# 64-row score matmuls of two experts side by side, three products of high and low parts, and eight buffers for turned probabilities

## The chip, the cores and the metric

The kernel runs on one core of one Trainium2 chip. The metric is device time in microseconds of one launch. TensorE (PE) multiplies, VectorE (DVE), ScalarE (ACT) and GpSimd (POOL) do the elementwise work, and SyncE (SP) issues the transfers.

## The reference, cut to what matters

Three stages follow each other on 2 batches of 768 tokens: a retention layer of 8 heads of 64, a channel MLP (512 to 2048 to 512), and a mixture of 4 attention experts of width 64. The change is in the last one:

```python
for e in range(E):                       # 4 experts, Hd = 64
    q = x @ wq[e]; k = x @ wk[e]; v = x @ wv[e]
    scores = scale * (q @ k.transpose(0, 2, 1))       # 768 x 768 for each batch
    scores = np.where(causal, -1000000000.0, scores)
    a = np.exp(scores - scores.max(-1, keepdims=True))
    a /= a.sum(-1, keepdims=True) + 1e-09
    ye = a @ v @ wo[e]
    # each token adds ye of its two best experts, weighted by the gate
```

## The kernel before

Matrix products keep more digits than one pass gives: an operand is split into a high part, rounded to the format that the program calls float32r, and the low part that is left, and products of parts are summed in PSUM.

In the attention stage `q_proj` (line 745) computes queries or keys of two experts (a pair p) for 384 tokens: 12 float32r matmuls of 128x384 in two groups of 6 (line 754). The 128 rows of the result are 64 of each expert. They leave by half-height instructions. For the queries ACT writes the high part into the expert's own 64 rows of a tile `QS` (line 764) and DVE the low part into the other 64 rows (line 766). For the keys ACT writes `KH` (771), DVE `KL` (773), and a DMA on SP copies each to the other 64 rows, so both halves hold the same.

`a_scores` (line 839) then makes the scores of one expert for 128 queries with matmuls over all 128 rows: `QS` against `KH` (line 861) and against `KL` (line 862), which sums all four products of parts. With nk = 128 to 768 keys there are 2 matmuls up to 512 keys, and 4 of half the width (320 or 384 columns) for 640 and 768. A score tile lies in one bank of PSUM (`ps1`) or two (`ps2`, three places). Behind it DVE masks the diagonal block (868) and finds the maximum (869), ACT takes the exponent with its sum (871), DVE inverts the sum (877, 878), and POOL scales by it and the gate (883). `a_turn` (889) transposes the 128x128 blocks on PE (903) and ACT or DVE copies them out (335) into `pt` or `ptn`. `a_value` multiplies by the values, two experts side by side in 64 columns each (922), and `a_out` applies the output weights (946). The value matmuls and transposes are plain float32, which the trace shows as two instructions for each value matmul and one for each transpose.

The retention stage has a similar form to the new one: at line 433 two heads are multiplied by 64-row float32 matmuls, one head in rows 0 to 63 and the other in rows 64 to 127.

The order on each engine isn't written out. `Plan.issue` lists the steps greedily: at each moment an engine that its own cost table calls free takes the waiting step of lowest priority number that has its inputs and whose buffers fit. So new costs and new buffer needs move the order of the whole attention stage.

Of the kernel before, what the change touches and what calls it, by code (L numbers as in the profile page):

```python
# [207 lines left out]
def region(base, size, n, space="S"):  # L208
    return [(space, base + i * size, size) for i in range(n)]
# [3 lines left out]
def retention_channel_mlp_mixture_attention(ctx: ExitStack, tc: tile.TileContext, a):  # L213
# [77 lines left out]
    x = o_h - 2 * (4 * KB + 16)  # L291
    PL["wv"] = PL["mraw"] = region(x, 4 * KB + 16, 2)
    PL["vraw"] = region(o_u, 4 * KB + 16, 1)
    PL["qk0"] = region(o_r, 3 * KB, 12)
    PL["vv0"] = region(o_r + 36 * KB, KB, 6)
    PL["ob"] = region(o_r + 42 * KB, 2 * KB, 2)
    PL["qk1"] = region(o_h, 3 * KB, 12)
    PL["vv1"] = region(o_h + 36 * KB, KB, 6)
    PL["pr"] = region(o_xt, 3 * KB, 8)
    PL["pt"] = region(o_x, 6 * KB, 3)  # L300
    PL["ptn"] = region(o_x, 7 * KB // 2, 5)
    PL["at"] = region(o_x + 18 * KB, 2 * KB, 3)
    PL["sm"] = region(o_sm, 16, 8)
    PL["mv"] = region(o_sm + 128, 16, 4)
# [10 lines left out]
    def new(n):  # L315
        return Buf(PL[n], n)
# [4 lines left out]
    def ACT(c, fn, r=(), w=()):  # L321
        P.add({"A": c}, lambda e: fn(), r, w)

    def DVE(c, fn, r=(), w=()):
        P.add({"V": c}, lambda e: fn(), r, w)
# [14 lines left out]
    def act_c(n):  # L340
        return 0.06 + n * 0.84e-3
# [391 lines left out]
        h, l, w = MW[n]  # L733
        return f32r(l if lo else h)[:, k * w + c0:k * w + c1]

    QS, KH, KL, VV, LG, GT = {}, {}, {}, {}, {}, {}
    xkeys = lambda t: [(t, "k", k) for k in range(NK)]

    def q_alloc(b):
        for e in range(E):  # L740
            QS[b, e], KH[b, e], KL[b, e] = (new(f"qk{b}") for _ in range(3))
        for t in range(NC):
            VV[b, t] = new(f"vv{b}")

    def q_proj(b, j, n, p):
        cs = slice(j * TB, (j + 1) * TB)
        pa = new("ps")
        xh, xl = XH[b][j], XL[b][j]
        for hf in range(2):
            def mm(hf=hf):  # L750
                i = 6 * hf
                for k in (2 * hf, 2 * hf + 1):
                    for lo, xt in ((0, xh), (0, xl), (1, xh)):
                        pe.matmul(f32(pa, TB), lhsT=mw(n, lo, k, p * 128, (p + 1) * 128), rhs=blk(f32r(xt))[:, k],  # L754
                                  start=(i == 0), stop=(i == 11))
                        i += 1
            PE(0.98, mm, r=list(MW[n][:2]) + xkeys(xh) + xkeys(xl) + ["seven"], w=[pa])
        for z in range(2):
            e = 2 * p + z
            own = slice(64 * z, 64 * z + 64)  # L760
            oth = slice(64 - 64 * z, 128 - 64 * z)
            if n == "wq":
                q = QS[b, e]
                ACT(0.39, lambda q=q, own=own: act.activation(f32r(q)[own, cs], f32(pa, TB)[own], AF.Copy, scale=0.125),
                    r=[pa], w=[(q, j, 0)])
                DVE(0.47, lambda q=q, own=own, oth=oth: dve.scalar_tensor_tensor(
                    f32r(q)[oth, cs], f32(pa, TB)[own], 0.125, f32(q)[own, cs], op0=OP.mult, op1=OP.subtract),
                    r=[pa, (q, j, 0)], w=[(q, j, 1)])
            else:
                kh, kl = KH[b, e], KL[b, e]  # L770
                ACT(0.39, lambda t=kh, own=own: act.activation(f32r(t)[own, cs], f32(pa, TB)[own], AF.Copy),
                    r=[pa], w=[(kh, j, 0)])
                DVE(0.47, lambda t=kl, h=kh, own=own: dve.tensor_tensor(f32r(t)[own, cs], f32(pa, TB)[own],
                                                                        f32(h)[own, cs], OP.subtract),
                    r=[pa, (kh, j, 0)], w=[(kl, j, 0)])
                for t in (kh, kl):
                    DMA(96e3, lambda t=t, own=own, oth=oth: sp.dma_start(f32(t)[oth, cs], f32(t)[own, cs]),
                        r=[(t, j, 0)], w=[(t, j, 1)])

    def q_val(b, t):  # L780
        j, cc = divmod(t, TPB)
# [57 lines left out]
    def a_scores(b, qt, p):  # L839
# [2 lines left out]
        sm = new("sm")  # L842
        PR = []
        P.bias -= (20, 40)[b]
        for z in range(2):
            e = 2 * p + z
            s, pr = new("ps2" if nk > 512 else "ps1"), new("pr")
            PR.append(pr)

            ways = 1 if nk <= 512 else 2  # L850
            wide = nk // ways

            def halves(ap, step):
                return ap[:, :ways * step].rearrange("p (a x) -> p a x", a=ways)[:, :, :wide]

            def mm(e=e, s=s):
                q = f32r(QS[b, e])[:, qt * C:(qt + 1) * C]
                for n in range(ways):
                    ks = slice(n * wide, (n + 1) * wide)
                    out = f32(s)[:, 512 * n:512 * n + wide]  # L860
                    pe.matmul(out, lhsT=q, rhs=f32r(KH[b, e])[:, ks], start=True, stop=False)  # L861
                    pe.matmul(out, lhsT=q, rhs=f32r(KL[b, e])[:, ks], start=False, stop=True)  # L862
            PE(2 * ways * max(0.107, wide * .4513e-3 + .015), mm, r=[(QS[b, e], j, 0), (QS[b, e], j, 1)] +
               [(t, jj, y) for t in (KH[b, e], KL[b, e]) for jj in range(j + 1) for y in range(2)], w=[s])

            def mx(s=s, z=z):
                end = 512 * (ways - 1) + wide
# [239 lines left out]
```

## Time and profile before

| | |
|---|---|
| three runs | 452.94, 453.08, 454.92 us, median 453.08 |
| profiled execution, its own time | 452.99 us |
| its span | 451.0 us |
| PE, PE's weight loads | 440.5 us, 416.2 us (98%, 92%) |
| DVE, ACT, POOL | 328.2, 223.3, 209.0 us (73%, 50%, 46%) |

The attention stage runs from 329.9 us to the end. A matmul's recorded duration includes the filling of a pipeline, so matmuls overlap in the records: what one costs PE is the distance from its start to the next one's start, called its step here. Start and duration of a row are its first two numbers.

### The profile page before, as it was taken

The page shows a single profiled execution, that of the slowest core. Times are in us where ns is not written, and L with a number is a line of the kernel's source. Part 1 is how long each engine was busy: PE and PEld are TensorE (multiplying, and loading weights), DVE is VectorE, ACT ScalarE, POOL GpSimd, SP SyncE. Part 2 cuts the span into 40 slices and gives each one's busy share as a digit, 9 for nine tenths or more (in the row PEclk, how much of TensorE's full clock was granted, in tenths as well). Part 3 has the DMA queues.
Part 4 walks back from the last instruction along what each step waited for, and adds up shares of the span by engine and source line. Part 5 has one row for each costly group of instructions (what it writes and reads, how often), then busy time and mean ns, then how long its engine had stood idle before and what let it go on. Part 6 is the DMA issues. An engine that isn't in the chain of part 4 may idle for free.

```text
span 451.0 us, 8469 instructions
## 1 busy us (share of the span) xinstructions
PE 440.5 (98%) x3200; PEld 416.2 (92%) x3200; DVE 328.2 (73%) x709; ACT 223.3 (50%) x467; POOL 209.0 (46%) x216
## 2 busy tenths in 40 slices
PE   8999999999999999999999999999999999999996
PEld 7778889999999999999999999999999987897885
DVE  2798786868659867876868665569657988878962
ACT  1477467164256336344354164244534756645852
POOL 1688768978989315326145064100401333224440
PEclk9999999999999999999999999999999999999999
DMA  7998923203104103114021002002230221101111
GB/s 267 331 366 322 322 69 124 94 8 133 47 1 140 48 1 120 68 48 139 2 89 53 1 1 93 2 0 95 70 72 18 66 67 39 49 1 47 49 49 47
DMA packets 14985, 40.11 MB, mean 89 GB/s; under 512 B 2272, under 2 KB 4960, under 8 KB 14944
## 3 DMA queue, kind: packets, MB, share of 16 engines
q1 hardware_dynamic: 14944, 39.57, 25.7%
q8 instruction: 25, 0.41, 0.4%
q14 instruction: 16, 0.13, 0.1%
HBM read 33.27 MB, written 3.15 MB: 81 GB/s over the span
## 4 chain that ended last, share of the span: by engine, by line
PE 86%; DVE 7%; POOL 2%; issue 1%; ACT 1%; DMA 1%; SPq 0%; DVEq 0%; ACTq 0%; POOLq 0%
PE ps L609 29%; PE ps L670 19%; PE ps L590 7%; PE ps L754 6%; PE ps L922 4%; PE ps L791 4%; PE ps L903 4%; PE ps L946 3%; PE ps L461 2%; PE ps L484 2%; PE ps L861 2%; PE ps L862 2%; PE ps L433 1%; DVE sm L869 1%; DMA vk<-in_vk_dram 1%
## 5 line engine op out<-in xcount | busy, mean ns | idle before, releaser
L609 PE MATMUL ps<-h,w 128*128 128x384 f32 x768 | 145.6, 335 | 0.7 <-DVE xT L613 0.4
L609 PEld LDWEIGHTS ps<-h,w 128*128 128x128 f32 x768 | 134.0, 188 | 1.4 <-DVE xT L613 0.7
L613 DVE TENSOR_TENSOR xT<-xT,ps 128x384 f32<-128x384 f32 x112 | 60.2, 550 | 36.9 <-PE ps L609 36.5
L883 POOL TENSOR_SCALAR pr<-pr,sm,gate 128x384 f32<-128x384 f32 (+5 forms) x48 | 34.7, 733 | 80.7 <-DVE ps L868 33.0
L546 POOL TENSOR_TENSOR w<-wy,w 128x512 fp32r<-128x512 f32 x26 | 33.6, 1297 | 44.3 <-PE ps L609 39.7
L670 PE MATMUL ps<-t,S 128*128 128x384 f32 x216 | 43.1, 334 | 0.0
L871 ACT ACTIVATE pr<-ps,sm 128x384 f32<-128x384 f32 (+5 forms) x48 | 30.4, 636 | 20.7 <-DVE sm L869 15.4
L677 ACT ACTIVATE u<-ps 128x384 f32<-128x384 f32 x36 | 17.6, 490 | 41.5 <-PE ps L670 35.8
L670 PEld LDWEIGHTS ps<-t,S 128*128 128x128 f32 x216 | 37.9, 188 | 0.1
L521 ACT ACTIVATE wx<-raw 128x512 f32<-128x512 f32 x32 | 21.5, 672 | 27.8 <-DVE ps L525 19.7
L590 PE MATMUL ps<-x,w 128*128 128x384 f32 x192 | 34.9, 336 | 0.4 <-ACT wx L521 0.4
L590 PEld LDWEIGHTS ps<-x,w 128*128 128x128 f32 x192 | 33.2, 188 | 0.8 <-ACT wx L521 0.6
L869 DVE TENSOR_REDUCE sm<-ps 128x1 f32<-128x384 f32 (+5 forms) x48 | 30.0, 625 | 2.9
L670 PE MATMUL ps<-x,w 128*128 128x384 f32 x144 | 28.8, 334 | 0.0
L685 ACT ACTIVATE h<-ps 128x384 fp32r<-128x384 f32 x36 | 17.6, 490 | 22.5 <-PE ps L609 14.4
L522 POOL TENSOR_SCALAR wx<-wx 128x512 f32<-128x512 f32 x32 | 20.1, 629 | 18.5 <-ACT wx L521 17.8
L670 PEld LDWEIGHTS ps<-x,w 128*128 128x128 f32 x144 | 25.3, 188 | 0.0
L545 ACT ACTIVATE w<-wy 128x512 fp32r<-128x512 f32 x26 | 16.3, 629 | 16.4 <-PE ps L609 16.1
L903 PE MATMUL ps<-ident,pr 128*128 128x128 f32 x168 | 22.4, 274 | 2.0 <-DVE at L933 1.1
L523 DVE TENSOR_SCALAR ps<-wx 128x512 uint32<-128x512 uint32 x32 | 22.0, 688 | 2.2 <-POOL wx L522 1.8
L527 DVE SCALAR_TENSOR_TENSOR wy<-raw,ps 128x512 uint32<-128x512 uint32 x32 | 21.8, 683 | 1.9 <-POOL w L546 1.3
L525 DVE SCALAR_TENSOR_TENSOR ps<-wx,ps 128x512 uint32<-128x512 uint32 x32 | 22.3, 695 | 1.1
(123 smaller groups left out, 878.4 us busy)
## 6 DMA issues: line engine op xcount, KB each, us to landing
raw<-in_w_dram SPq DMA_DIRECT2D x32, 512.0 KB, 3.4
vk<-in_vk_dram SPq DMA_DIRECT2D x12, 512.0 KB, 5.8
kq<-in_kq_dram SPq DMA_DIRECT2D x11, 512.0 KB, 5.7
qk<-qk SPq DMA_DIRECT2D x32, 96.0 KB, 2.1
out_dram<-ob SPq DMA_DIRECT2D x11, 256.0 KB, 2.0
tabY<-in_tabY_dram SPq DMA_DIRECT2D x6, 256.0 KB, 4.9
vraw<-in_wv_dram SPq DMA_DIRECT2D x1, 520.0 KB, 3.3
kq<-in_kq_dram SPq DMA_DIRECT2D x2, 256.0 KB, 3.0
```

What stands on the lines that cost most here:

```text
L523: DVE(0.62, lambda: dve.tensor_scalar(u32(z), u32(x), 4, 1, op0=OP.logical_shift_left, op1=OP.logical_shift_right), r=[x], w=[z])
L525: DVE(0.7, lambda: dve.scalar_tensor_tensor(u32(z), u32(x), 0x80000000, u32(z), op0=OP.bitwise_and, op1=OP.bitwise_or), r=[x, z], w=[z])
L546: POOL(1.34, lambda: pool.tensor_tensor(f32r(l), f32(y), f32(h), OP.subtract), r=[y, h], w=[l])
L590: pe.matmul(f32(pa, TB), lhsT=wt, rhs=blk(f32r(xt[b][j]))[:, k], start=(n == 0), stop=(n == 11))
L609: pe.matmul(f32(pa, TB), lhsT=wt, rhs=t, start=(n == 0), stop=(n == 5))
L613: DVE(0.55, lambda: dve.tensor_tensor(blk(f32(xt))[:, k], blk(f32(xt))[:, k], f32(pa, TB), OP.add), r=[pa] + [(xt, cc, w) for cc in range( ...
L670: pe.matmul(f32(pa, TB), lhsT=wt, rhs=t, start=(first and n == 0), stop=(n == 5), skip_group_check=True)
L754: pe.matmul(f32(pa, TB), lhsT=mw(n, lo, k, p * 128, (p + 1) * 128), rhs=blk(f32r(xt))[:, k], start=(i == 0), stop=(i == 11))
L869: dve.tensor_reduce(f32(sm)[:, z:z + 1], halves(f32(s), 512), axis=mybir.AxisListType.XY, op=OP.max, negate=True)
L871: ACT(act_c(nk) + .18, lambda s=s, pr=pr, z=z: act.activation(halves(f32(pr), wide), halves(f32(s), 512), AF.Exp, bias=f32(sm)[:, z:z + 1] ...
L883: POOL(0.28 + nk * 0.95e-3, lambda pr=pr, z=z, e=e: pool.tensor_scalar(f32(pr, nk), f32(pr, nk), f32(sm)[:, 6 + z:7 + z], GT[b, j][:, cc, ...
L903: pe.transpose(f32(pa)[:, i * C:(i + 1) * C], f32(PRS[z][x])[:, j * C:(j + 1) * C], ident)
```

## The change

`q_proj` leaves a pair by one full-height ACT instruction (high) and one full-height DVE instruction (low), for queries and keys alike; expert z stays in rows 64z to 64z+63. The copies by DMA are gone. `a_scores` computes both experts of a pair in one step of PE: for each of three products (high-high, low-high, high-low; low-low is dropped) one 64-row matmul for each expert, alternating, each into its own score tile. The step takes both score tiles at once, where before each expert took its own. Query and key tiles shrink from 12 to 8 places, and the places for `ptn` grow from 5 to 8 out of that.

```diff
--- before.py
+++ after.py
@@ -291,14 +291,14 @@
     x = o_h - 2 * (4 * KB + 16)
     PL["wv"] = PL["mraw"] = region(x, 4 * KB + 16, 2)
     PL["vraw"] = region(o_u, 4 * KB + 16, 1)
-    PL["qk0"] = region(o_r, 3 * KB, 12)
+    PL["qk0"] = region(o_r, 3 * KB, 8)
     PL["vv0"] = region(o_r + 36 * KB, KB, 6)
     PL["ob"] = region(o_r + 42 * KB, 2 * KB, 2)
-    PL["qk1"] = region(o_h, 3 * KB, 12)
+    PL["qk1"] = region(o_h, 3 * KB, 8)
     PL["vv1"] = region(o_h + 36 * KB, KB, 6)
     PL["pr"] = region(o_xt, 3 * KB, 8)
     PL["pt"] = region(o_x, 6 * KB, 3)
-    PL["ptn"] = region(o_x, 7 * KB // 2, 5)
+    PL["ptn"] = region(o_x, 7 * KB // 2, 5) + region(o_r + 24 * KB, 7 * KB // 2, 3)
     PL["at"] = region(o_x + 18 * KB, 2 * KB, 3)
     PL["sm"] = region(o_sm, 16, 8)
     PL["mv"] = region(o_sm + 128, 16, 4)
@@ -733,12 +733,13 @@
         h, l, w = MW[n]
         return f32r(l if lo else h)[:, k * w + c0:k * w + c1]
 
-    QS, KH, KL, VV, LG, GT = {}, {}, {}, {}, {}, {}
+    QK, VV, LG, GT = {}, {}, {}, {}
     xkeys = lambda t: [(t, "k", k) for k in range(NK)]
 
     def q_alloc(b):
-        for e in range(E):
-            QS[b, e], KH[b, e], KL[b, e] = (new(f"qk{b}") for _ in range(3))
+        for p in range(2):
+            for n in ("wk", "wq"):
+                QK[n, b, p] = new(f"qk{b}"), new(f"qk{b}")
         for t in range(NC):
             VV[b, t] = new(f"vv{b}")
 
@@ -755,27 +756,15 @@
                                   start=(i == 0), stop=(i == 11))
                         i += 1
             PE(0.98, mm, r=list(MW[n][:2]) + xkeys(xh) + xkeys(xl) + ["seven"], w=[pa])
-        for z in range(2):
-            e = 2 * p + z
-            own = slice(64 * z, 64 * z + 64)
-            oth = slice(64 - 64 * z, 128 - 64 * z)
-            if n == "wq":
-                q = QS[b, e]
-                ACT(0.39, lambda q=q, own=own: act.activation(f32r(q)[own, cs], f32(pa, TB)[own], AF.Copy, scale=0.125),
-                    r=[pa], w=[(q, j, 0)])
-                DVE(0.47, lambda q=q, own=own, oth=oth: dve.scalar_tensor_tensor(
-                    f32r(q)[oth, cs], f32(pa, TB)[own], 0.125, f32(q)[own, cs], op0=OP.mult, op1=OP.subtract),
-                    r=[pa, (q, j, 0)], w=[(q, j, 1)])
-            else:
-                kh, kl = KH[b, e], KL[b, e]
-                ACT(0.39, lambda t=kh, own=own: act.activation(f32r(t)[own, cs], f32(pa, TB)[own], AF.Copy),
-                    r=[pa], w=[(kh, j, 0)])
-                DVE(0.47, lambda t=kl, h=kh, own=own: dve.tensor_tensor(f32r(t)[own, cs], f32(pa, TB)[own],
-                                                                        f32(h)[own, cs], OP.subtract),
-                    r=[pa, (kh, j, 0)], w=[(kl, j, 0)])
-                for t in (kh, kl):
-                    DMA(96e3, lambda t=t, own=own, oth=oth: sp.dma_start(f32(t)[oth, cs], f32(t)[own, cs]),
-                        r=[(t, j, 0)], w=[(t, j, 1)])
+        hi, lo = QK[n, b, p]
+        c = 0.125 if n == "wq" else 1.0
+        ACT(act_c(TB), lambda: act.activation(f32r(hi)[:, cs], f32(pa, TB), AF.Copy, scale=c), r=[pa], w=[(hi, j)])
+        if n == "wq":
+            DVE(dve_c(TB), lambda: dve.scalar_tensor_tensor(f32r(lo)[:, cs], f32(pa, TB), c, f32(hi)[:, cs],
+                                                            op0=OP.mult, op1=OP.subtract), r=[pa, (hi, j)], w=[(lo, j)])
+        else:
+            DVE(dve_c(TB), lambda: dve.tensor_tensor(f32r(lo)[:, cs], f32(pa, TB), f32(hi)[:, cs], OP.subtract),
+                r=[pa, (hi, j)], w=[(lo, j)])
 
     def q_val(b, t):
         j, cc = divmod(t, TPB)
@@ -842,26 +831,26 @@
         sm = new("sm")
         PR = []
         P.bias -= (20, 40)[b]
+        ways = 1 if nk <= 512 else 2
+        wide = nk // ways
+        SS = [new("ps2" if nk > 512 else "ps1") for _ in range(2)]
+        (kh, kl), (qh, ql) = QK["wk", b, p], QK["wq", b, p]
+
+        def halves(ap, step):
+            return ap[:, :ways * step].rearrange("p (a x) -> p a x", a=ways)[:, :, :wide]
+
+        def mm():
+            for n in range(ways):
+                for i, (x, y) in enumerate(((qh, kh), (ql, kh), (qh, kl))):
+                    for z in range(2):
+                        zs = slice(64 * z, 64 * z + 64)
+                        pe.matmul(f32(SS[z])[:, 512 * n:512 * n + wide], lhsT=f32r(x)[zs, qt * C:(qt + 1) * C],
+                                  rhs=f32r(y)[zs, n * wide:(n + 1) * wide], start=(i == 0), stop=(i == 2))
+        PE(3 * ways * max(0.107, wide * .4513e-3 + .015) + 0.15, mm,
+           r=[(qh, j), (ql, j)] + [(t, jj) for t in (kh, kl) for jj in range(j + 1)], w=SS)
         for z in range(2):
-            e = 2 * p + z
-            s, pr = new("ps2" if nk > 512 else "ps1"), new("pr")
+            s, pr = SS[z], new("pr")
             PR.append(pr)
-
-            ways = 1 if nk <= 512 else 2
-            wide = nk // ways
-
-            def halves(ap, step):
-                return ap[:, :ways * step].rearrange("p (a x) -> p a x", a=ways)[:, :, :wide]
-
-            def mm(e=e, s=s):
-                q = f32r(QS[b, e])[:, qt * C:(qt + 1) * C]
-                for n in range(ways):
-                    ks = slice(n * wide, (n + 1) * wide)
-                    out = f32(s)[:, 512 * n:512 * n + wide]
-                    pe.matmul(out, lhsT=q, rhs=f32r(KH[b, e])[:, ks], start=True, stop=False)
-                    pe.matmul(out, lhsT=q, rhs=f32r(KL[b, e])[:, ks], start=False, stop=True)
-            PE(2 * ways * max(0.107, wide * .4513e-3 + .015), mm, r=[(QS[b, e], j, 0), (QS[b, e], j, 1)] +
-               [(t, jj, y) for t in (KH[b, e], KL[b, e]) for jj in range(j + 1) for y in range(2)], w=[s])
 
             def mx(s=s, z=z):
                 end = 512 * (ways - 1) + wide
```

What this does to the order on PE, first in batch 0 between the projections: `x` and `wk`, `wq` are inputs and weights of a projection, `qk0` are queries and keys of batch 0, `ps` is PSUM. Before:

```order
L754 MATMUL ps_71<-x_47_341,wk_470_3107 128x384
L754 MATMUL ps_71<-x_44_327,wk_472_3118 128x384
L861 MATMUL ps_71<-qk0_505_3477,qk0_513_3526 128x384
L862 MATMUL ps_71<-qk0_509_3494,qk0_513_3526 128x384
L754 MATMUL ps_71<-x_44_327,wk_470_3107 128x384
L754 MATMUL ps_71<-x_47_341,wk_470_3107 128x384
```

After, where "x2" is one 64-row matmul for each expert:

```order
L755 MATMUL ps_71<-x_47_341,wq_473_3126 128x384
L755 MATMUL ps_71<-x_44_327,wq_474_3135 128x384
L847 MATMUL ps_71<-qk0_504_3474,qk0_509_3508 128x384 x2
L847 MATMUL ps_71<-qk0_504_3474,qk0_510_3510 128x384 x2
L847 MATMUL ps_71<-qk0_506_3478,qk0_509_3508 128x384 x2
L755 MATMUL ps_71<-x_44_327,wq_473_3126 128x384
L755 MATMUL ps_71<-x_47_341,wq_473_3126 128x384
```

One expert's two matmuls became six for both experts, and they stand between matmuls over all 128 rows on both sides.

The last scores of the program on PE (batch 1, queries 640 to 767, second pair), before and after. `qk1` are queries and keys of batch 1, `at` the attention result that the output weights `wo` (L946, L935) multiply, `pr` probabilities that are transposed:

```order
L861 MATMUL ps_71<-qk1_531_3786,qk1_544_3864 128x384
L862 MATMUL ps_71<-qk1_548_3885,qk1_544_3864 128x384
L861 MATMUL ps_71<-qk1_531_3786,qk1_544_3864 128x384
L862 MATMUL ps_71<-qk1_548_3885,qk1_544_3864 128x384
L946 MATMUL ps_71<-wo_500_3434,at_647_4746 128x512
L946 MATMUL ps_71<-wo_501_3445,at_647_4746 128x512
```

```order
L847 MATMUL ps_71<-qk1_524_3736,qk1_536_3820 128x384 x2
L847 MATMUL ps_71<-qk1_524_3736,qk1_539_3829 128x384 x2
L847 MATMUL ps_71<-qk1_535_3818,qk1_536_3820 128x384 x2
L892 MATMUL ps_71<-ident_63,pr_631_4664 128x128
L892 MATMUL ps_71<-ident_63,pr_636_4710 128x128
L892 MATMUL ps_71<-ident_63,pr_631_4664 128x128
```

Before, 12 output matmuls follow the last scores; now transposes of earlier probabilities follow at once, and the output matmuls stand ahead of the scores. Counted over the attention stage, PE changes between matmuls over 128x128, over 64 columns (L922) and over 64 rows 18 times before and 54 times after: 22 times to 64 rows (6 of these from 64 columns), 10 times to 64 columns, 11 to transposes and 11 to other 128-row matmuls. Before it was 9 times to 64 columns, 8 to other 128-row matmuls and once to transposes.

The same place on DVE: masks (COPY_PREDICATED) and maxima (TENSOR_REDUCE into `sm`) of these last scores, and copies of transposed blocks into `pt`. Before:

```order
L868 COPY_PREDICATED ps_71<-future_69,negs_70 128x128
L869 TENSOR_REDUCE sm_650_4771<-ps_71 128x1
L868 COPY_PREDICATED ps_71<-future_69,negs_70 128x128
L869 TENSOR_REDUCE sm_650_4771<-ps_71 128x1
L335 COPY ob_654_4799<-ps_71 128x512
L877 TENSOR_SCALAR sm_650_4771<-sm_650_4771 128x2
L878 RECIPROCAL sm_650_4771<-sm_650_4771 128x2
L335 COPY pt_655_4805<-ps_71 128x512
L335 COPY pt_656_4824<-ps_71 128x512
L335 COPY pt_656_4824<-ps_71 128x384
```

After:

```order
L857 COPY_PREDICATED ps_71<-future_69,negs_70 128x128
L858 TENSOR_REDUCE sm_644_4785<-ps_71 128x1
L857 COPY_PREDICATED ps_71<-future_69,negs_70 128x128
L858 TENSOR_REDUCE sm_644_4785<-ps_71 128x1
L335 COPY pt_647_4814<-ps_71 128x512 x2
L866 TENSOR_SCALAR sm_644_4785<-sm_644_4785 128x2
L867 RECIPROCAL sm_644_4785<-sm_644_4785 128x2
L922 TENSOR_TENSOR at_649_4840<-ps_71,at_649_4840 128x256
L335 COPY pt_650_4847<-ps_71 128x512
```

In both, the two masks and maxima stand ahead of the copies into `pt`; now the two copies for the second expert follow them directly.

## Rows read from the trace of the kernel before

**Rows 1.** Page, busy us of each engine (share of the span), instructions

```profile
PE 440.5 (98%) x3200; PEld 416.2 (92%) x3200; DVE 328.2 (73%) x709; ACT 223.3 (50%) x467; POOL 209.0 (46%) x216
```

**Rows 2.** Waits of PE, 329 to 451 us: total us, times, longest

```profile
PE ps L903 <- DVE at L933: 1.1, 1, 1.1
PE ps L903 <- ACT pt L335: 0.6, 1, 0.6
PE ps L903 <- DVE pt L335: 0.3, 1, 0.3
PE ps L861 <- ACT pr L871: 0.2, 1, 0.2
```

**Rows 3.** Busy us by stretch: PE, weight loads, DVE, ACT, POOL; granted clock

```profile
415.00:430.00 15.00, 13.67 (x99) 11.26 (x98) 13.58 (x36) 12.39 (x30) 8.18 (x10) 1.00 0.10 37
```

**Rows 4.** Timeline of PE from 379 us: start, us, line, shape, count

```profile
379.41 0.28 PE L862 MATMUL ps<-qk,qk 128*128 128x128 f32 x1
379.52 0.33 PE L861 MATMUL ps<-qk,qk 128*128 128x256 f32 x1
379.69 0.28 PE L862 MATMUL ps<-qk,qk 128*128 128x256 f32 x1
...
380.05 1.21 PE L754 MATMUL ps<-x,wq 128*128 128x384 f32 x6
```

**Rows 5.** Timeline of PE from 414 us

```profile
414.71 0.40 PE L862 MATMUL ps<-qk,qk 128*128 128x512 f32 x1
414.95 0.31 PE L861 MATMUL ps<-qk,qk 128*128 128x320 f32 x1
...
415.39 0.31 PE L862 MATMUL ps<-qk,qk 128*128 128x320 f32 x1
416.80 0.63 PE L903 MATMUL ps<-ident,pr 128*128 128x128 f32 x4 [1.10 <-DVE at L933]
```

**Rows 6.** Timeline of PE, 359.8 to 366.8 us, changes between 128 and 64 columns

```profile
360.28 0.49 PE L903 MATMUL ps<-ident,pr 128*128 128x128 f32 x3
360.70 1.74 PE L922 MATMUL ps<-ptn,vv 128*64 128x256 f32 x16
362.36 0.45 PE L861 MATMUL ps<-qk,qk 128*128 128x384 f32 x1
362.65 0.34 PE L862 MATMUL ps<-qk,qk 128*128 128x384 f32 x1
...
363.00 0.34 PE L862 MATMUL ps<-qk,qk 128*128 128x384 f32 x1
363.26 1.74 PE L922 MATMUL ps<-ptn,vv 128*64 128x256 f32 x16
```

**Rows 7.** Timeline of PE from 30.6 us, into the retention's 64-row pairs

```profile
30.61 0.66 PE L484 MATMUL ps<-ident,xT 128*128 128x128 f32 x4
31.19 1.16 PE L433 MATMUL ps<-kq 64*128 64x128 f32 x16
```

**Rows 8.** The same from 31.96 us, the last eight (four pairs) and the next

```profile
31.74 0.61 PE L433 MATMUL ps<-kq 64*128 64x128 f32 x8
32.28 0.44 PE L484 MATMUL ps<-ident,xn 128*128 128x128 f32 x2
```

**Rows 9.** Groups by line and shape: busy us, mean ns; idle before, releasers

```profile
L773 DVE TENSOR_TENSOR qk<-ps,qk 64x384 fp32r<-64x384 f32 x16 | 8.9, 554 | 4.7 <-ACT qk L771 4.3
L868 DVE COPY_PREDICATED ps<-future,negs 128x128 f32<-128x128 uint32 x48 | 17.3, 360 | 1.2 <-PE ps L862 0.5 <-PE ps L861 0.5
L869 DVE TENSOR_REDUCE sm<-ps 128x1 f32<-128x768 f32 x8 | 7.7, 958 | 0.5
L871 ACT ACTIVATE pr<-ps,sm 128x768 f32<-128x768 f32 x8 | 7.2, 901 | 5.0 <-DVE sm L869 5.0
L335 DVE COPY pt<-ps 128x512 f32<-128x512 f32 x6 | 4.1, 685 | 0.4 <-PE ps L903 0.3
```

## The prediction

> **What bounds the kernel now.** I read the page's busy times first, then the waits of PE in the attention stage, then the timeline of PE there, and last the groups by shape. The page shows PE busy for 98% of the span, no other engine above 73% [rows 1]. Busy could still mean waiting matmuls, so the next view is who waits: in the whole attention stage PE has four waits, 1.1, 0.6, 0.3 and 0.2 us, 2.2 together [rows 2]. The timeline shows what one costs: from 415.39 to 416.80 are 1.41 us where a step of that shape is 0.15, so 1.26 are lost where the view says 1.1 [rows 5]. With the same 0.16 on each of the four I count 2.9 us (an estimate). The rest is a dense stream: what changes there is what PE issues, and nearly all of it shows in the time. DVE is the engine behind PE: busy 13.58 of 15 us in a late stretch [rows 3], so a later DVE can still hold PE up. The granted clock of that stretch is 1.00, the 2.4 GHz level [rows 3]; PE stays as busy as now, and I put nothing on the clock.
>
> **The score stream: what it removes.** Steps of the 128-row score matmuls, from start to start: 128 columns 0.11 us (379.41 to 379.52), 256 columns 0.12 (three steps from 379.69 to 380.05) [rows 4]; 512 columns 0.24 (414.71 to 414.95), 320 columns 0.147 (three steps, 414.95 to 415.39) [rows 5]; 384 columns 0.175 (two steps from 362.65 to 363.00) [rows 6]. For 2 batches, 4 experts and 6 query tiles there are 16, 16, 32, 48 and 16 matmuls of 128, 256, 320, 384 and 512 columns. That is 1.76 + 1.92 + 4.70 + 8.40 + 3.84 = 20.6 us now. Afterwards three products replace two for each expert, but the two experts share a step if their 64-row halves run at once: three quarters of as many steps, 15.5 us.
>
> Do the halves run at once? The retention's 64-row pairs say so for float32: four pairs (eight instructions) from 31.74 to 32.28 take 0.54 us [rows 8]. Of it 0.09 is the change of shape at the end (next paragraph but one), so a pair costs 0.1125 us, where a single 128-row transpose costs 0.11 (three from 360.28 to 360.70, less the same 0.09) [rows 6]. That is 1.02 times one step for two matmuls. On it the new stream is 15.5 x 1.02 = 15.8 us: **4.8 to 5.1 us less, I take 5.0**. The other bound is no overlap of float32r halves at all: 31.0 us, 10.4 more than now. I take the near end, since the row is the same form of matmul, though not the same number format.
>
> The Trainium skill, "TensorE: Matmul & The Clock Gate", section "Measured speedup vs the span model", gives four row tiles of 32 rows 3.07 times the throughput of one, not four times. By it, as an estimate, a pair would cost about 1.3 steps. The trace disagrees for its float32 pairs, at 1.02 [rows 8]; the page's rule is kept as a rival below.
>
> **The changes of shape: what it adds.** PE pays when a matmul of another row or column shape follows. From 363.00 to 363.26 a 384-column step takes 0.26 instead of 0.175 before a 64-column matmul: 0.09 us of emptying [rows 6]. Then the first matmul of the new shape is late by a lead that depends on what it loads. Into 128-row float32r: 362.36 to 362.65 is 0.29 for a 0.175 step, 0.11 [rows 6]. Into 64 rows: 31.19 to 31.74 is 0.55 for four pairs of 0.1125, 0.10 [rows 7, 8]. Into transposes: 30.61 to 31.19 is 0.58 for four steps of 0.11 and 0.09 of emptying, 0.05 [rows 7]; the same 0.05 is taken into 64 columns.
>
> The order gives the counts. Before, 18 changes: 18 x 0.09 + (9 + 1) x 0.05 + 8 x 0.11 = 3.0 us. After, 54: 54 x 0.09 + 22 x 0.10 + (11 + 10) x 0.05 + 11 x 0.11 = 4.86 + 2.20 + 1.05 + 1.21 = 9.3 us. **The added 36 changes cost 6.3 us**, more than the stream saves. A block that stands alone between 128-row matmuls, as in batch 0 between the projections, pays 0.09 + 0.10 + 0.09 + 0.11 = 0.39 us; a 384-key block goes from four steps (0.70) to three (0.53) and so loses 0.22. Only the largest, eight steps of 0.175, get back 0.35 and nearly break even. The bounds: a change that falls into a wait of PE costs nothing, so 0 if all were covered; with PE waiting only 2.9 us in all, most can't be, and I take them in full.
>
> The Trainium skill, "TensorEngine Tiling (Array Packing)", section "Key Properties", says it outright: changing the tiling mode drains the engine. That speaks against this change, and the trace agrees, with 0.09 us of emptying [rows 6].
>
> **Evacuations and transfers: off the path.** Sixteen projections each lose one of two DVE instructions and one of two ACT instructions. The half-height DVE subtraction takes 0.554 [rows 9]; if height doesn't matter, DVE is relieved of 16 x 0.554 = 8.9 us, if time went with height, of nothing. ACT is relieved likewise. The cover is PE's stream, so neither counts directly; what it can give is less waiting below. The 32 copies between halves, and the wait of the first scores for them, go too: PE has projections to do there and shows no wait for them [rows 2].
>
> **Waits.** Now 2.9 us. The change pulls both ways. DVE gets lighter, and eight `ptn` places let transposes go ahead. Against that, the step of scores needs two free score tiles at once, and the tail loses cover. At the tail the order lets me work it out. Let T be the end of the last scores. Before, 12 output matmuls fill PE behind T. After, 22 transposes follow, then the value matmuls of the first pair, which need the second expert's `pt` copy on DVE. On DVE two masks and maxima stand ahead: 2 x (0.36 + 0.96) = 2.6 us, then the copy, 0.685 [rows 9], so about T + 3.4 with a tenth for the handing over. PE is through its transposes at T + 0.09 + 0.05 + 22 x 0.11 = T + 2.56. So PE waits 0.9 to 1.0 us where it had none. For the rest of the stage I take 1.0 us, between nothing (DVE relieved) and all of today's 2.9; together **2.0 us in place of 2.9, 0.9 less**.
>
> **Sum.** -5.0 + 6.3 - 0.9 = +0.4 us. The profiled execution took 452.99 us in its own time (span 451.0 and 2.0 around it), within 0.1 of the median of the three runs; so 453.4, and 453.5 against the median.
>
> **Rivals.**
> Slower, by paired score tiles: PE can't start a 640- or 768-key block until the first expert's tile of the block before is free, 0.36 + 0.96 + 0.90 = 2.2 us behind that block's end [rows 9]. There are eight such blocks; in the new order other PE work of roughly 2.3 us or more stands between them, which just covers it. It decides if DVE gets to them over a microsecond late, as its 13.58 of 15 us allow [rows 3]: four blocks at 1.1 us add 4.4 less the 1.0 already counted, 457. Against it: DVE is relieved by up to 8.9 us.
> Slower, by pairs that overlap in part or not: the pairs in the trace are float32, whose 128-column step of 0.11 equals what float32r needs for 128, but float32r moves 256 columns in 0.12 [rows 4], so the overlap is shown only at about half the column rate. At 1.3 steps a pair the stream is 20.2 us, 0.4 saved instead of 5.0: 458.1. With none it is 453.5 + 15.4 = 468.9.
> Faster, by covered changes: all of the counted waits go as DVE is relieved (-2.0), and half of the added changes fall where PE would have stood anyway (-3.1): 448.4. For it: the four waits of today stand before or after scores or transposes, where shapes now change. Against it: 2.2 us of waiting in a stage of 120 us leaves little to hide in.
> That the change doesn't do what it says, three quarters of the steps, is the second of these at its far end.
>
> **How the numbers follow.** The forecast has 0.61: its stream and counts are fixed to some 0.5 us, its waits lie between 0 and 4, so 451.5 to 455.5 is its own range. Paired tiles 0.13, pairs that don't overlap 0.10, covered changes 0.16. A measurement of this kernel can tell about 0.5% from no change, 2.3 us: faster is under 450.8, slower over 455.3. Of the forecast 0.02 falls under, 0.07 over, 0.52 between. Covered changes give 0.14 to faster and 0.02 to the same; the two others are slower. Faster 0.16, same 0.54, slower 0.30. The range from 450.0 to 457.8 leaves out about 0.10 on each side: the faster half of the covered changes, and the pairs with their overlap at 1.3 or worse.
>
> **What would show it right or wrong.** In the changed profile, two 64-row score matmuls start within 0.01 us of each other and pairs of 384 columns follow at 0.175 to 0.185; at 0.35 they don't overlap. The first pair behind a projection starts about 0.09 late, its second 0.10 more. The waits of PE sum to about 2 us, with one of about 1 us before value matmuls near the end. DVE's busy time falls by 8 to 9 us with no gain from it. The prediction is wrong if the distance at changes of shape is that of an ordinary step, if steps of pairs are much over one step, or if PE's waits leave 0 to 4 us.

## The result: 5.2 us slower, outside the predicted range

The changed kernel takes 458.3 us (median of four runs, 458.08 to 458.52) against 453.12 us for the kernel before on the same chip: 1.0108 times as long, interval 1.0093 to 1.0123. The prediction was 453.5 us within 450.0 to 457.8, "no change" its likeliest case.

The page of the profile after, busy us of each engine as in [rows 1]:

```profile
PE 443.4 (97%) x3264; PEld 411.9 (90%) x3264; DVE 320.5 (70%) x697; ACT 212.6 (47%) x447; POOL 209.2 (46%) x216
```

PE is busy for 2.9 us more, DVE 7.7 us and ACT 10.7 us less, and the span grew from 451.0 to 456.1. So the two engines that got lighter gave nothing to the time, and PE's busy time explains only part of the 5.1 us.

I took the loss apart by the starts of matmuls. Both kernels end with the same matmuls but for the scores, so I go from the 950th matmul before the end (1014th after, 64 more scores), at 310.85 and 310.87 us, to the last one's start. Each matmul gets its step, each change of shape its price (both as in the prediction; its prices as printed give 3.0 and 9.3 for the changes, 0.1 and 0.2 less than stands here), and what is left of the distance is called waits:

| us | before | after | difference | predicted |
|---|---|---|---|---|
| distance | 136.0 | 141.2 | +5.2 | +0.4 |
| steps of the scores | 20.5 | 15.7 | -4.8 | -5.0 |
| all other steps | 108.8 | 108.8 | 0 | 0 |
| changes of shape (18, 54) | 3.1 | 9.5 | +6.5 | +6.3 |
| waits, what is left | 3.7 | 7.2 | +3.5 | -0.9 |

The rows for steps and changes are counts times steps and prices taken from the kernel before, so the table alone doesn't test them; the trace after does. A block of 768 keys and what follows it, PE's timeline after from 361.7 us (start, duration, line, shape, count):

```profile
362.21 1.32 PE L847 MATMUL ps<-qk,qk 64*128 64x384 f32 x12
363.46 0.44 PE L911 MATMUL ps<-ptn,vv 128*64 128x256 f32 x2
```

From 362.21 to 363.46 are 1.25 us: a lead of 0.10, six pairs of 0.175 and 0.09 of emptying make 1.24. So a pair of 64-row float32r matmuls takes what one matmul over 128 rows took [rows 6], and the price of a change is the one that the rows of before gave. Over the whole distance the median step of a 384-column pair is 0.175 us, and the steps at and just behind the 54 changes lie 0.004 us over their printed price in the median (worked out from the starts in the trace). So two terms came out as forecast.

The third term failed. The waits of PE after, 329 to 457 us, as in [rows 2]:

```profile
PE ps L892 <- ACT ptn L335: 1.4, 1, 1.4
PE ps L847 <- ACT pr L860: 0.7, 1, 0.7
PE ps L911 <- DVE ptn L335: 0.7, 1, 0.7
PE ps L911 <- ACT ptn L335: 0.6, 1, 0.6
PE ps L911 <- ACT pt L335: 0.5, 1, 0.5
PE ps L935 <- DVE at L922: 0.3, 1, 0.3
PE ps L892 <- DVE ob L335: 0.2, 1, 0.2
```

They sum to 4.4 us where four waits summed to 2.2 [rows 2]; the view counts idle time alone, so less than the table. By stretch, with the columns of [rows 3] (the last two are the DMA share and GB/s):

```profile
385.00:400.00 15.00, 15.00 (x125) 12.61 (x122) 11.11 (x44) 6.63 (x21) 2.85 (x6) 1.00 0.05 19
400.00:415.00 15.00, 12.90 (x103) 9.24 (x103) 12.42 (x47) 10.69 (x36) 6.47 (x12) 0.89 0.05 19
415.00:430.00 15.00, 13.79 (x94) 10.23 (x92) 11.14 (x31) 6.94 (x17) 5.79 (x8) 1.00 0.19 71
430.00:445.00 15.00, 13.79 (x114) 10.34 (x111) 11.20 (x24) 8.92 (x21) 6.23 (x7) 1.00 0.10 37
```

and two stretches of before in which PE never stood ([rows 3] has the one between them):

```profile
400.00:415.00 15.00, 15.00 (x111) 12.61 (x110) 13.13 (x52) 8.98 (x31) 5.46 (x10) 1.00 0.10 36
430.00:445.00 15.00, 15.00 (x136) 12.67 (x135) 7.85 (x15) 7.04 (x16) 3.71 (x4) 1.00 0.10 37
```

Between 400 and 415 PE now stands for 2.1 of 15 us and between 430 and 445 for 1.2, where it stood for nothing; from 415 to 430 it stands for 1.2 as against 1.3. In the worst stretch DVE, which I had feared as the engine that is late, is at 12.42, less than before; ACT has gone from 8.98 to 10.69, and neither is full. PE waits for engines that are not saturated. PE's timeline after says where (in brackets idle time and its releaser):

```profile
402.08 0.96 PE L847 MATMUL ps<-qk,qk 64*128 64x128 f32 x12
402.97 0.55 PE L892 MATMUL ps<-ident,pr 128*128 128x128 f32 x3
404.93 0.55 PE L892 MATMUL ps<-ident,pr 128*128 128x128 f32 x3 [1.41 <-ACT ptn L335]
405.40 0.79 PE L847 MATMUL ps<-qk,qk 64*128 64x384 f32 x6
...
407.61 1.65 PE L847 MATMUL ps<-qk,qk 64*128 64x512 f32 x6
409.19 0.88 PE L892 MATMUL ps<-ident,pr 128*128 128x128 f32 x3
...
411.86 2.82 PE L911 MATMUL ps<-ptn,vv 128*64 128x256 f32 x32 [0.58 <-ACT ptn L335]
414.61 0.98 PE L847 MATMUL ps<-qk,qk 64*128 64x512 f32 x6
415.52 3.03 PE L935 MATMUL ps<-wo,at 128*128 128x512 f32 x12
```

The twelve score matmuls at 402.08 are two blocks, one of 128 and one of 256 keys, for both experts: four score tiles within 0.9 us. The four masks and maxima follow one after the other on DVE, the first of them:

```profile
403.11 0.43 DVE L857 COPY_PREDICATED ps<-future,negs 128x128 f32<-128x128 uint32 x1
403.65 0.29 DVE L858 TENSOR_REDUCE sm<-ps 128x1 f32<-128x128 f32 x1
```

and on ACT the exponent that waits for that maximum stands ahead of the copy that PE needs:

```profile
404.04 0.37 ACT L860 ACTIVATE pr<-ps,sm 128x128 f32<-128x128 f32 x1 [1.84 <-DVE sm L858]
...
404.39 0.48 ACT L335 ACTIVATE ptn<-ps 128x384 f32<-128x384 f32 x1
```

So ACT stands for 1.84 us with the copy queued behind the exponent, and PE for 1.41 behind the copy. Among the blocks with large tiles, where I had put this rival, stand one wait for a score tile, 0.7 before a 320-column step, and two for copies, 0.7 and 0.5; the longest wait is at small blocks.

In that run the granted clock was 0.5, the 1.2 GHz level, from 406.5 to 409.9 us, 1.6 us after the wait of 1.41 had ended: the 512-key block at 407.61 takes 1.58 us to the next start, the one at 414.61 takes 0.91. What that is worth is taken up with the eleventh experiment.

### The profile page after: what moved, and what is told of

The parts are those of the page before. It is cut to its first block, busy times and chain, and to the rows that moved or that the text cites. A ratio compares the mean times of both kernels' runs of the same rounds, so it can differ in the third digit from the quotient of the medians.

```text
span 456.1 us, 8472 instructions
## 1 busy us (share of the span) xinstructions
PE 443.4 (97%) x3264; PEld 411.9 (90%) x3264; DVE 320.5 (70%) x697; ACT 212.6 (47%) x447; POOL 209.2 (46%) x216
## 4 chain that ended last, share of the span: by engine, by line
PE 87%; DVE 3%; DMA 3%; ACT 2%; issue 2%; POOL 1%; SPq 0%; DVEq 0%; ACTq 0%; POOLq 0%
PE ps L609 28%; PE ps L670 18%; PE ps L755 8%; PE ps L590 7%; PE ps L911 4%; PE ps L780 4%; PE ps L847 4%; PE ps L892 3%; PE ps L935 3%; DMA vk<-in_vk_dram 2%; PE ps L484 2%; PE ps L461 2%; PE ps L433 2%; DMA out_dram<-ob 1%; PE ps L468 1%
## 5 line engine op out<-in xcount | busy, mean ns | idle before, releaser
L892 PEld LDWEIGHTS ps<-ident,pr 128*128 128x128 f32 x168 | 19.0, 144 | 5.1 <-ACT ptn L335 2.3
```

The lines of the kernel that those rows point to most:

```text
L892: pe.transpose(f32(pa)[:, i * C:(i + 1) * C], f32(PRS[z][x])[:, j * C:(j + 1) * C], ident)
```

## The experiments

The theory: the extra waits come from the score step that needs the places of both experts at once. The rivals: what else the change moves, that is the 36 added changes themselves, the output tiles, the lighter evacuations, the extra `ptn` places or the planner's wrong cost. Each ratio is to the kernel before as run beside it (453.16 to 453.39 us). Except in the first, sixth and eleventh experiment the edit makes the planner order the attention stage anew. "Waits" and "changes" are those of the table above (before 3.7 and 3.1, after 7.2 and 9.5).

**1. The change without changes of shape.** The two experts aren't separated: each product is one matmul over all 128 rows, into one tile or the other.

```diff
-                    for z in range(2):
-                        zs = slice(64 * z, 64 * z + 64)
-                        pe.matmul(f32(SS[z])[...], lhsT=f32r(x)[zs, ...], rhs=f32r(y)[zs, ...],
-                                  start=(i == 0), stop=(i == 2))
+                    z = i % 2
+                    pe.matmul(f32(SS[z])[...], lhsT=f32r(x)[:, ...], rhs=f32r(y)[:, ...],
+                              start=(i < 2), stop=(i > 0))
```

> The changed kernel with its order kept, but each of the three products is one 128-row matmul (alternately into the first and the second expert's score tile) in place of two 64-row ones: as many steps of PE, no change to the 64-row shape; what is left out is the separation of the two experts, so the scores are other numbers. Changes of shape fall from 54 to 20, 9.5 us to 3.4 by the rows' prices. Theory A (changes of shape are paid in full on top of the waits): 458.3 - 6.1 = 452.2, waits of PE stay near 7 us. Rival B (PE is held by the softmax anyway, so that what is taken from PE comes back as waiting): 455 to 458, waits of PE over 10 us.

454.12 us, 1.0018 (1.0003 to 1.0032): 4.2 us less than after. The changes fall from 9.5 to 3.4, but the waits rise from 7.2 to 8.9, the longest 1.7 us again for ACT's `ptn` copy. So the price of the changes is real, and 1.8 of its 6.1 us comes back as waiting. The waits don't come from the changes: without them PE waits longer. (What this kernel leaves out is the separation of the experts, so its scores are other numbers; its order of steps is that of after.)

**2. Before, with paired tiles.** The old 128-row matmuls, four products and all, but one PE step for both experts that takes both tiles.

```diff
+        SS = [new("ps2" if nk > 512 else "ps1") for _ in range(2)]
-            PE(2 * ways * max(...), mm, r=[(QS[b, e], j, 0), ...], w=[s])
+        PE(4 * ways * max(...), mm, r=[(QS[b, e], j, y) for e in E2 for y in range(2)] + [...], w=SS)
```

> The kernel before with one edit: the scores of both experts of a pair are one step of PE that takes both score tiles at once (same 128-row matmuls, same number, copies and half-height instructions as before). Theory A (waits come from taking the tiles in pairs: coarser score steps, the tail without output matmuls behind the last scores): 453.1 + 3 to 4 = 456 to 457, PE waits 6 to 7 us, with one near 1 us before the last value matmuls but one. Rival B (pairing is harmless, the waits come from changes of shape that the planner's costs don't see, or from the lighter evacuations): 452.5 to 454.

457.17 us, 1.0088 (1.0073 to 1.0103), 4.0 us slower than before, with 20 changes (3.3 us) and the same stream: all of it is waits, 7.7 us. PE's waits there, 329 to 457 us:

```profile
PE ps L859 <- ACT pr L874: 2.6, 3, 1.0
PE ps L949 <- DVE at L936: 0.5, 1, 0.5
PE ps L925 <- ACT pt L335: 0.5, 1, 0.5
PE ps L906 <- POOL pr L886: 0.4, 1, 0.4
PE ps L906 <- DVE ptn L335: 0.2, 1, 0.2
```

The largest group is the score step itself (L859) waiting until an exponent has emptied a tile. One of the three on PE's timeline:

```profile
413.54 0.34 PE L859 MATMUL ps<-qk,qk 128*128 128x384 f32 x1
...
414.24 0.82 PE L906 MATMUL ps<-ident,pr 128*128 128x128 f32 x6
416.04 0.50 PE L859 MATMUL ps<-qk,qk 128*128 128x512 f32 x1 [0.98 <-ACT pr L874]
```

Scores of a 512-key and a 384-key block, two tiles each, stand in front of it; the third block's step can't start until a tile is emptied, however little else is to do. This part of the change alone costs at least what the whole change loses in waits, though its waits end on score tiles where most of those of after end on copies. The Trainium skill, "TensorEngine Tiling (Array Packing)", section "Gotcha 1: PSUM Pressure", says that row tiling adds to the pressure on PSUM; it gives no size. Here the joined step with its need for both experts' tiles, on matmuls over all 128 rows, is 4.0 us; what the 64-row form itself adds to the pressure no run shows.

**3. Before, with the second tile only held.** As the second, but each expert keeps its own step; the first one's step reserves the second's tile.

```diff
+        SS = [new("ps2" if nk > 512 else "ps1") for _ in range(2)]
-               [(t, jj, y) for t in (KH[b, e], KL[b, e]) ...], w=[s])
+               [(t, jj, y) for t in (KH[b, e], KL[b, e]) ...], w=[s], hold=SS)
```

> The kernel before with one edit smaller than in e2: the two experts keep a score step each, but the first expert's step already takes (holds) the second's score tile. It parts the two halves of e2, which alone moved the time from 453.2 to 457.2. Theory A (what costs is that two free score tiles are needed before a step can stand): 455.5 to 457, PE waits 6 to 7 us. Rival B (what costs is the joint step, which keeps the first mask back until both experts' matmuls are through): 452.5 to 454, PE waits near 3 us.

455.86 us, 1.0054 (1.004 to 1.0069): 2.5 of the 4.0 us. Needing the second place early is the larger part; that both experts' scores then come in one piece is the rest, 1.5.

**4 and 5. Before, paired only for large or only for small blocks.** The edit of the second, for 640 and 768 keys (`joint = nk > 512`) or for up to 512 (`joint = nk <= 512`).

```diff
+        joint = nk > 512
+        if joint:
+            scores((0, 1))
         for z in range(2):
+            if not joint:
+                scores((z,))
```

> The edit of e2 (both experts' scores in one step, both tiles taken at once, on the kernel before) for the eight blocks of 640 and 768 keys only. Theory A (the prediction's slower rival had the right place: the two-bank tiles, of which there are three): 455.5 to 457, most of e2's 4.0 us. Rival B (the small blocks at the start of batch 1, where the changed trace waits longest, carry it): 453 to 454.5.

> The same edit for the blocks of up to 512 keys only. Theory A of e22 (two-bank tiles carry the cost): 453 to 454.5. Rival B (the small blocks carry it): 455.5 to 457. If the two parts of e2 add up, this and e22 together stand 4.0 over twice 453.2.

454.8 us, 1.0048 (1.0026 to 1.007), and 454.49 us, 1.0025 (1.0012 to 1.0038): 1.6 and 1.3 us by the medians. (The first ratio is higher than its median says, as two of its eight runs took 456.54 and 458.4 us.) By the intervals the large blocks cost 1.2 to 3.2 us and the small ones 0.5 to 1.7, so neither size of tile carries the loss alone, and whether the two parts add up to 4.0 can't be told.

**6. After, with six output tiles.** One wait of the change is DVE's for an output tile (1.20 us at 423.81, until a transfer out had landed).

```diff
-    PL["ob"] = region(o_r + 42 * KB, 2 * KB, 2)
+    PL["ob"] = region(o_r + 42 * KB, 2 * KB, 2) + region(o_h + 24 * KB, 2 * KB, 4)
```

> The changed kernel with six places for the output tiles in place of two, the order on PE being the same. In the changed trace DVE stands 1.2 us at 423.8 for an output transfer that still reads its tile, and PE waits 0.2 and 0.7 us for DVE behind it. Theory A (that wait is on the path): 458.3 - 0.9 = 457.4. Rival B (the same waits come a step later from masks and maxima): 458.3, within 0.3.

457.68 us, 1.0103 (1.0088 to 1.0118), 0.6 us less than after by the medians, waits 6.9. But this edit changes nothing. The planner takes the first place of its list that it counts free, the four new ones stand last, and it counts a place free sooner than the transfer leaves it (some 3.1 us after the issue by its own table; the transfer that DVE waited for took 4.5). The plan has the order and the places of after, and DVE waits for the same transfer still:

```profile
424.02 0.69 DVE L335 COPY ob<-ps 128x512 f32<-128x512 f32 x1 [0.88 <-DMA out_dram<-ob]
```

So this is the changed kernel run again, and the 0.6 us are a measure of scatter: differences of that size between runs of the new form mean nothing. The ninth run answers the question instead. There that transfer has landed in time, the same copy waits for PE,

```profile
423.66 0.69 DVE L335 COPY ob<-ps 128x512 f32<-128x512 f32 x1 [0.69 <-PE ps L935]
```

and PE stands behind DVE for 0.94 us all the same, where it stood for 0.21 and 0.68 in after. The output tiles are not what PE waits for.

**7. After, with the planner told of the price.** Its cost of a score step has 0.15 us for the changes; a lone block pays 0.39.

```diff
-        PE(3 * ways * max(0.107, wide * .4513e-3 + .015) + 0.15, mm,
+        PE(3 * ways * max(0.107, wide * .4513e-3 + .015) + 0.40, mm,
```

> The changed kernel with one number in the planner's cost of a score step changed, 0.15 to 0.40 us, which is near what two changes of shape cost in the trace (0.39). Only the order changes (51 changes of shape in place of 54, 9.1 us). Theory A (the order is wrong because the planner is blind to the changes): waits of PE fall from 7 to 4 us or less, 454.5 to 455.5. Rival B (the waits come from paired tiles and the softmax chain, whatever the cost table says): 457.5 to 459.

458.81 us, 1.0129 (1.0114 to 1.0144): no better. There are 51 changes instead of 54 (9.1 us) and the waits are 7.6: with the price in its cost table the planner still hardly groups the blocks.

**8. After, leaving the projections in half-height pieces.** Two ACT and two DVE instructions again for each projection; the copies by DMA stay away.

```diff
-        ACT(act_c(TB), lambda: act.activation(f32r(hi)[:, cs], ...), r=[pa], w=[(hi, j)])
+        for z in range(2):
+            own = slice(64 * z, 64 * z + 64)
+            ACT(act_c(TB), lambda own=own: act.activation(f32r(hi)[own, cs], ...), r=[pa], w=[(hi, j, z)])
```

> The changed kernel with its projections leaving by half-height instructions again, two on ACT and two on DVE for each (no copies by DMA). DVE gets 8.9 us more work, ACT 7.8. Theory A (these engines are off the path, as in the prediction): within 1.0 of 458.3. Rival B (the lighter DVE has kept the waits of the changed kernel from being longer): 460 to 463, PE waits 9 us or more.

458.83 us, 1.0113 (1.0091 to 1.0136): 0.5 us more than after by the medians, which is inside the scatter. The time doesn't tell all: the order planned for it has 49 changes of shape in place of 54, some 0.9 us less, and its waits by the table's measure are 9.2 us, 2.0 more than after, one of them 1.57 us for a scaling on POOL at 409.36. So the heavier evacuations do seem to lengthen the waits, and the order that came with them hides it. What relieving DVE and ACT buys is small in the time and not cleanly separated by this run.

**9. After, with six `ptn` places in place of eight.**

```diff
-    PL["ptn"] = ... + region(o_r + 24 * KB, 7 * KB // 2, 3)
+    PL["ptn"] = ... + region(o_r + 24 * KB, 7 * KB // 2, 1)
```

> The changed kernel with six places for the turned probabilities in place of eight (with five the planner finds no order). Theory A (the added places are there to make an order possible and buy no time): within 0.5 of 458.3. Rival B (they let transposes go ahead of the values): 459.5 to 461.

457.85 us, 1.0094 (1.0074 to 1.0114), with 55 changes and waits 6.9: the added places buy no time that shows.

**10. After, with a fifth bank for one-bank score tiles** (`PL["ps1"] = banks[:5]`), and **a run without the scores' lead** (their priority no longer moved ahead by 20 and 40):

> The changed kernel with five single-bank places for score tiles of up to 512 keys in place of four (the fifth is shared with transposes). Theory A (pairs of tiles are what is short where these blocks stand, 400 to 415 us): PE waits fall by 1 to 3 us, 455.5 to 457.5. Rival B (the fifth bank is taken from the transposes' copies, or the softmax engines bound that place): 458 to 460.

> The changed kernel without the planner's lead for score steps (priority numbers lowered by 20 and 40 become 0): scores are planned in their program order, 49 changes of shape in place of 54 (8.8 us). Theory A (the lead was tuned for single-expert steps; another order brings the waits of the paired form down): 455 to 457. Rival B (scores come later, the softmax chain of a group is then uncovered): 459 to 464.

460.25 us, 1.0144 (1.0127 to 1.0161), and 464.76 us, 1.0261 (1.0229 to 1.0294). Both are worse. With five banks the waits are 8.7, 1.0 of it now for DVE's copies to output tiles; the fifth bank is also one of the pool `psa` (line 308), so it isn't an added place. Without the lead they are 13.4, and 4.4 of them are scores behind an exponent:

```profile
PE ps L847 <- ACT pr L860: 4.4, 4, 1.7
```

I read this as pairs that ask for early scores and for free tiles at once, of which neither setting gives both; a lead between 0 and the present one, or a larger one, was not tried.

**11. After, three products of one expert, then three of the other.** The loops over products and experts are swapped.

```diff
-                for i, (x, y) in enumerate(((qh, kh), (ql, kh), (qh, kl))):
-                    for z in range(2):
+                for z in range(2):
+                    for i, (x, y) in enumerate(((qh, kh), (ql, kh), (qh, kl))):
```

> The changed kernel with the six 64-row matmuls of a score step in another sequence: the three of the first expert, then the three of the second, so that neighbours use the same 64 rows; the counts, tiles and the order of steps stay. Theory A (the stream's gain comes from two halves of rows running at once, which needs them to alternate): the score stream goes from 15.7 to about 28 to 31 us and the time to 468 to 474. Rival B (PE overlaps them whatever the sequence, or 64-row matmuls are cheaper one by one): within 3 of 458.3.

458.21 us, 1.0106 (1.0082 to 1.0131): no difference, so alternating isn't what the gain needs. The trace from 363.2 us, the same block as above:

```profile
363.27 1.32 PE L847 MATMUL ps<-qk,qk 64*128 64x384 f32 x12
364.52 0.65 PE L911 MATMUL ps<-ptn,vv 128*64 128x256 f32 x4
```

1.25 us for twelve matmuls again, and they start in pairs (0.010 us apart, the next pair a step later), not one by one at half a step. The halves run side by side in this sequence too.

Its clock stayed at 1.00 where that of after fell, with the same stall before it:

```profile
400.00:415.00 15.00, 12.67 (x108) 9.54 (x106) 12.42 (x47) 10.45 (x35) 6.90 (x13) 1.00 0.09 33
```

Its waits are 6.3 us by the table's measure, 0.9 less than in the profiled run of after. Order and places are the same, so by this pair some 0.9 of the 3.5 us there is the half clock, and 2.6 are waits at full clock. (Summed step by step in the stretch itself the half clock costs 1.5 us; some of it comes back as shorter waits.) In the four runs of after it doesn't show: the one with a mean clock of 1.000 took 458.52 us, the one at 0.994 took 458.43. In two other kernels it does: in the ninth experiment the runs at 0.998 and 0.999 took 457.4 us and those at 0.995 and 0.996 458.3 and 458.6, and in the first the three at 0.999 to 1.000 took 453.0 to 454.0, the five at 0.994 to 0.996 454.0 to 454.8. How much of the medians' 5.2 us the clock makes is open, about 1 us at most by these.

## Why the prediction was wrong

**The score stream: right.** 4.8 us less where 4.8 to 5.1 stood and 5.0 was taken. The transfer from float32 pairs to float32r pairs held: the rival "pairs that overlap in part or not" is out, with 1.25 us for six pairs and two changes.

**The changes of shape: right in price and number.** 54 of them, 6.5 us more where 6.3 stood. That most of them can't hide is shown by the first experiment from the other side: without them 4.2 of 6.1 us come off the time. The faster rival, covered changes, asked for half; about three tenths are covered, but by waits that the change brings with it.

**Evacuations and transfers: right in size.** DVE is relieved of 7.7 us (8.9 estimated), since a full-height subtraction takes what a half-height one took [rows 9]:

```profile
L763 DVE SCALAR_TENSOR_TENSOR qk<-ps,qk 128x384 fp32r<-128x384 f32 x6 | 3.3, 550 | 3.3 <-ACT qk L761 3.2
```

That it gives the time little fits the eighth experiment, which moved by 0.5 us; that it leaves the waits as they are does not, as they were 2.0 us longer there.

**Waits: the step that failed.** "For the rest of the stage I take 1.0 us, between nothing (DVE relieved) and all of today's 2.9; together 2.0 us in place of 2.9, 0.9 less." By the prediction's own count (the view's idle time and 0.16 us for each wait) 2.9 us became 5.5, 2.6 more; by the table they rose by 3.5, of which some 0.9 is the half clock. The bound itself was wrong: it let today's waits be the most that could be, though the paragraph named the step that needs two free tiles at once. A new need for places isn't bounded by the waits of the old order. The second experiment, which is that need in a joined step and nothing else of the change, makes 4.0 us, and the need alone 2.5. That the same need makes the waits of the changed kernel is concluded from this and from the rivals that fell (the changes of shape, the `ptn` places, the output tiles, the planner's cost); no run of the changed kernel takes its tiles one by one, so there it is not shown directly. All of it holds for this planner with its leads of 20 and 40. The tail, which I did work out, is the small part: 0.9 to 1.0 us expected (its terms give 0.84), 0.47 found at 441.10, because ACT and not DVE made the last copy that it waited for.

**The clock** was put at nothing because PE would stay as busy as now. It didn't, and the granted clock fell in six of eight profiled kernels with the 64-row pairs; that is the smaller miss.

**The rival "slower, by paired score tiles"** had the mechanism, 457 us, and 0.13 of the chance. Its place was half of it, and its condition was wrong, so that 457 lies near the result is in part luck. It looked at the blocks of 640 and 768 keys alone, where the small ones cost as well (fourth and fifth experiment), and asked whether DVE would be a microsecond late for them. In the trace DVE is busy for less than before, and the longest wait stands at small blocks, where two pairs fill four tiles in under a microsecond and the queues of DVE and ACT then hand them back one by one. I read the pressure from the busy share of an engine; at that wait it lay in the places and the order in the queues.

The sum with its terms as measured: -4.8 + 6.5 + 3.5 = +5.2 us. None of the runs has a median under that of the kernel before. A lone block pays 0.39 us for its two changes and saves a quarter of its steps, so by these prices (an estimate) the three-product form breaks even only from some nine 384-column steps on, and the largest block has eight.

## What to carry to other kernels

Where a change makes one step out of two, count the places that the joined step needs at its start and what must be handed back before it, and price that as a wait of its own; today's waits bound nothing there. Test it on the old kernel by joining the allocation alone, before anything else is rewritten. When an experiment adds places, look in its trace for whether they were taken. And a matmul of another shape that saves a quarter of its steps must come in long enough runs to pay for entering and leaving that shape.

## What the hardware did that I had not expected

PE doesn't keep the program's order between the two halves of its rows. In the eleventh run the program lists three matmuls of one half before those of the other, and yet a second matmul starts 0.010 us after the first one of a block, where with alternation it is 0.003 us. The records don't name the rows; that the two of a pair belong to different halves is inferred from the six steps that twelve matmuls took.

In six of the eight profiled kernels with 64-row pairs the granted clock fell to the 1.2 GHz level between 405 and 414 us, for 3.4 us in five of them (406.5 to 409.9 in after) and 6.8 us in the run without the scores' lead, each time within 3 us behind a wait of PE of 0.7 to 1.6 us. The eleventh run waited 1.39 us at the same place and the first experiment's 1.71, and their profiled runs kept 2.4 GHz.
